# An attention and two-MoE kernel: its first step issued as one hand-ordered piece, with bias rows made on chip

## The chip, the cores and the metric

The kernel runs on one core of a Trainium2 chip. Five engines work in parallel: TensorE (PE in the profile, its weight loads PEld), VectorE (DVE), ScalarE (ACT), GpSimd (POOL) and SyncE (SP), which here issues nearly all transfers. The metric is the device time of one execution in microseconds, lower is better. All data is float32, and the kernel has one launch.

## What is computed

```python
scores = scale * np.matmul(q, k.transpose(0, 1, 3, 2))      # 4 batches, 8 heads, 576 x 576, head dim 64
cum = np.cumsum(np.maximum(s, 0.0), axis=-1)
bias = -(cum[:, :, :, None] - cum[:, :, None, :])
scores = np.where(causal, -1e9, scores + np.minimum(bias, 0.0))
attn = exp(scores - max) / (sum + 1e-9)
x = matmul(attn, v)                                          # then 2304 tokens x 512
h = maximum(maximum(x @ w1, x @ w2), x @ w3) ; x = h @ w_out         # 768 wide
out = ((x @ w_a) * (x @ w_b)) @ w_out2                               # 1536 wide
```

## The kernel before

Attention goes in eight steps: four batches, each in two halves (R = 0: the first 256 query rows, R = 1: the other 320). A step has four pairs of heads; "pair 0" to "pair 3" are those of step 0, "pair 4" to "pair 7" those of step 1, "pair 8" and "pair 9" the first two of step 2. The first three steps are "plain": scores are one matmul of 66 contraction rows, 64 of the head and two that carry the bias. Row 64 of the key operand holds the running sums of `s` (`cum`) and row 65 a constant; the query operand has a constant and `cum`. The host packs the 66-row arrays (`kq0`, `k1`, `q1`) with the constants and a dummy row, and the kernel overwrites the dummy rows.

For one head of step 0 the work is: two score matmuls into a PSUM bank (`f`, line 631), mask and row minimum on VectorE (line 563), exponential with sum on ScalarE (570), two small VectorE operations (574, 575), the division on GpSimd (580), three transposes on TensorE (`ft`, 673), a copy to SBUF (676), and for both heads together eight small matmuls with v (`fpv`, 698). The result is split into a high part on ScalarE (`Xh`, 81) and a low part on VectorE (`Xl`, 92). This is one "unit" of softmax per head, eight units in step 0. Step 1 has per pair one joint tile (`fj`) and four more score tiles.

The first MoE's gates (`g`, 762) follow one step behind: a gate of step 0 is 12 matmuls over the four pairs' `Xh` and `Xl`, so it needs all four. There are 18 weight tiles. Each is loaded as int64 words into `wraw` (512 KB; three buffers) and converted: a Prelu on ScalarE (248), a shift (251) and a combine (252) on VectorE, a copy on GpSimd (`hg`, 88) and a difference on VectorE (`lg`, 92).

The order on each engine is fixed at build time: code is traced in the order of a list of positions (`stream`), under priorities, and a list scheduler with a timeline places each instruction. Every engine then runs its own list in order, and waits where an operand isn't ready. In step 0 pairs 0 and 1 are loaded first, pairs 2 and 3 each behind the bias rows of the pair before (`rows_in`). Dummy matmuls (`spin`, 158) are put between.

Of the kernel before, what the change touches and what calls it, by code (L numbers as in the profile page):

```python
# [8 lines left out]
F32 = mybir.dt.float32  # L9
# [20 lines left out]
def kernel(  # L30
# [48 lines left out]
    def rnd(eng, o, i, scale=1.0):  # L79
        if eng == "A":  # L80
            nc.scalar.activation(o, i, AF.Copy, scale=scale)  # L81
        elif eng == "V":
            if scale == 1.0:
                nc.vector.tensor_copy(o, i)
            else:
                nc.vector.tensor_scalar_mul(o, i, scale)
        else:
            nc.gpsimd.tensor_scalar(o, i, scale, 1.0, op0=ALU.mult, op1=ALU.mult)  # L88

    def sub(eng, o, a, b):  # L90
        e = nc.vector if eng == "V" else nc.gpsimd
        e.tensor_tensor(o, a, b, op=ALU.subtract)
# [42 lines left out]
    SR = s.shape[0]  # L135
# [18 lines left out]
    def spin(n):  # L154

        ps = ps_m.tile([P, 512], F32, tag="m", name="spin")
        for _ in range(n):
            nc.tensor.matmul(ps[:, :P], ident, ident, start=True, stop=True)

    with tc.high_priority(5200):  # L160
        spin(16)

    with tc.high_priority(5000):
        ones = pt_tile([SR, 2, 4 * N1], F32, "ones")[:, 0, : 2 * S]
        cs = pt_tile([SR, 2, 4 * N1], F32, "cs")
        sraw, cum = cs[:, 0, : 2 * S], cs[:, 1, : 2 * S]
        nc.sync.dma_start(sraw, s)
        nc.vector.memset(ones[:, : 2 * S], 1.0)
        nc.vector.memset(ones[:, Q0 : Q0 + 1], 0.0)
        nc.vector.tensor_scalar_max(sraw[:, : 2 * Q0], sraw[:, : 2 * Q0], 0.0)  # L170
# [4 lines left out]
    nc.vector.tensor_scalar_max(sraw[:, 2 * Q0 :], sraw[:, 2 * Q0 :], 0.0)  # L175
    for h in range(2):
        c = slice(2 * Q0 + h * N1, 2 * Q0 + (h + 1) * N1)
        nc.vector.tensor_tensor_scan(
            cum[:, c], ones[:, c], sraw[:, c], cum[:, (h + 1) * Q0 - 1 : (h + 1) * Q0],
            op0=ALU.mult, op1=ALU.add,  # L180
        )

    def store_tails():
        chl = [
            mp.tile([SR, KC * N1], F32R, tag=f"X{c}1", bufs=1, name=f"c{c}")
            for c in "hl"
        ]
        nc.scalar.copy(chl[0][:, : 2 * S], cum)
        nc.gpsimd.tensor_tensor(
            chl[1][:, : 2 * S], cum, f(chl[0][:, : 2 * S]), op=ALU.subtract  # L190
        )
        for (dk, dq, t) in (
            (ck, cq, cum),
            (kt[:, 0], qt[:, 0], f(chl[0])),
            (kt[:, 1], qt[:, 1], f(chl[1])),
        ):
            a, b = parts(t)
            nc.sync.dma_start(dk[:, :, :Q0], a)
            nc.sync.dma_start(dk[:, :, Q0:], b)
            nc.sync.dma_start(dq[:, 0], b[:, 0])  # L200
            nc.sync.dma_start(dq[:, 1, 0:64], b[:, 1, 256:])
            nc.sync.dma_start(dq[:, 1, 64:], b[:, 1, :256])


    KB1 = ap_.tile([P, 2, S], F32R, name="KB1")
    KB2 = ap_.tile([P, 2, S], F32R, name="KB2")
    QA1 = ap_.tile([P, QW], F32R, name="QA1")
    QA2 = ap_.tile([P, QW], F32R, name="QA2")
# [4 lines left out]

    def preset():
        nc.gpsimd.memset(f(QA1[:, N1 : N1 + 64]), 0.0)
# [57 lines left out]
    w1_raw = {}  # L273

    def fetch_w1(key):
        raw = wst.tile([P, WC, 2], I32, tag="wst", name="wraw")
# [9 lines left out]
    def load_w1(key):  # L286
# [8 lines left out]
        with tc.issue_after(done_sm[-1][0]), tc.issue_after(done_sm[-1][1]):  # L295
# [165 lines left out]
    rows_in = []  # L461

    def load_pair(b, p, R):
# [9 lines left out]
        if b == 0 and p >= 2 and R == 0 and plain:  # L473
            t = vo_tile("kqv")[:, : MF * N1]
            kt_, qt_ = t[:, : 4 * Q0], t[:, 4 * Q0 :]
        else:
            kt_ = ap_.tile([P, WK], F32, tag="sk", bufs=2, name="kraw")
            qt_ = kt_ if own and plain else ap_.tile([P, WQV], F32, tag="sq", bufs=2, name="qvraw")
        kn = kt_[:, : 2 * nk]
        if plain and R == 0:  # L480
            qn, vn = kt_[:, 2 * nk : 4 * nk], qt_[:, : nb * P]
            nc.sync.dma_start(kt_[0:66, : 4 * nk], kq0[bp])
# [9 lines left out]
        if plain:  # L492
            if R:
                nc.sync.dma_start(kn[0:66], k1[bp])
                nc.sync.dma_start(qn[0:66], q1[bp])
                nc.sync.dma_start(kn[64:65], ck[bp : bp + 1])
                nc.sync.dma_start(qn[65:66], cq[bp : bp + 1])
            else:
                row = parts(cum)[0][bp : bp + 1] if b == 0 else ck[bp : bp + 1, :, :Q0]
                nc.sync.dma_start(kn[64:65], row)  # L500
                rows_in.append(nc.sync.dma_start(qn[65:66], row).ins)
            nc.sync.dma_start(vn, qv[b, p][:, 2 * nq :])
        else:
            if own:
                nc.sync.dma_start(qt_[:, : 2 * nq], qv[b, p][:, : 2 * nq])
                nc.sync.dma_start(vn, qv[b, p][:, 2 * nq :])
            else:
                nc.sync.dma_start(qt_[:, : 2 * nq + nb * P], qv[b, p])
            for r in (0, 64):
                nc.sync.dma_start(kn[r : r + 64], kT[b, p, :, :, 0:nk])  # L510
# [37 lines left out]
    def softmax(rows, pt, scale):  # L548


        n = len(rows)
        sm = small("sm", 2)
        rs = small("rs", 2)
        for g, parts in enumerate(rows):
            nm = small("nm", 2)
            first = 3.0e38
            for i, (v_, c0) in enumerate(parts):
# [5 lines left out]
                nc.vector.tensor_tensor_reduce(  # L563
# [9 lines left out]
            )  # L573
# [1167 lines left out]
```

## Time and profile before

| | us |
|---|---|
| median of 3 runs | 901.45 (901.07 to 904.96) |
| profiled execution, its own time | 903.33 |
| span of its instructions | 901.5 |
| TensorE busy in the span | 886.2 |
| VectorE busy | 624.9 |

The profiled execution is 1.88 us above the median; 1.83 us of its time lie around the span. TensorE is busy for 98% of the span, but that counts dummy matmuls, and matmuls at the lower of its two clock levels, as full work. The rows below show the first 44 us, where the two differ most from useful work, and the start of step 2 around 105 us.

### The profile page before, as it was taken

To read this page: it belongs to the slowest core of one execution; us is meant where nothing else is said; L and a number is where in the kernel's file an instruction comes from. 1 tells how busy PE (TensorE), PEld (TensorE's weight loads), DVE (VectorE), ACT (ScalarE), POOL (GpSimd) and SP (SyncE) were. 2 spreads that over 40 slices of the span, in tenths; PEclk is the share of its full clock that TensorE was granted. 3 is DMA by queue.
4 is the path that set the end of the run, shared out by engine and by line. 5 is a ranking of instruction groups with operands and counts; after the bars stand their busy time and mean duration, and the time that the engine had idled before them with its cause. 6 is when DMAs were issued, how large, how long until landed. Compare 5 with 4: busy or idle time off the path is not lost.

```text
span 901.5 us, 16886 instructions
## 1 busy us (share of the span) xinstructions
PE 886.2 (98%) x6098; PEld 840.1 (93%) x6098; DVE 624.9 (69%) x1427; ACT 392.8 (44%) x855; POOL 211.1 (23%) x324
## 2 busy tenths in 40 slices
PE   7999999999999999999999999999999999999998
PEld 6677699999999899889999999999999999999998
DVE  4786345677577666647587967767675868987874
ACT  3655455667556556535564322322222223433321
POOL 6552222324233322200001212111111210321211
PEclk8999899999999999999999999999999999999999
DMA  5665253336421873345501014444443245254231
GB/s 186 213 202 191 75 146 101 108 96 189 123 76 55 234 236 128 125 172 201 189 27 71 36 67 152 148 149 146 146 150 120 100 143 165 83 165 153 96 117 47
DMA packets 68267, 120.04 MB, mean 133 GB/s; under 512 B 7016, under 2 KB 50696, under 8 KB 68184
## 3 DMA queue, kind: packets, MB, share of 16 engines
q1 hardware_dynamic: 61272, 111.88, 38.1%
q10 hardware_dynamic: 6912, 7.08, 2.3%
q8 instruction: 48, 0.79, 0.4%
q14 instruction: 35, 0.29, 0.1%
HBM read 87.90 MB, written 31.01 MB: 132 GB/s over the span
## 4 chain that ended last, share of the span: by engine, by line
PE 89%; DMA 5%; DVE 2%; SPq 1%; issue 1%; ACT 1%; POOL 1%; ACTq 0%; DVEq 0%; POOLq 0%
PE X L1107 28%; PE g L762 22%; PE Z L1107 14%; PE Y L1107 7%; PE fpv L698 5%; PE t L714 3%; PE f L631 2%; PE s L587 2%; PE s L588 1%; PE W L1107 1%; PE ft L673 1%; PE tj L727 1%; PE sj L622 1%; PE sj L621 1%; DMA h1S<-st 1%
## 5 line engine op out<-in xcount | busy, mean ns | idle before, releaser
L762 PE MATMUL g<-Xh,lg 128*128 128x256 f32 (+1 forms) x576 | 173.8, 303 | 0.0
L762 PE MATMUL g<-Xh,hg 128*128 128x256 f32 (+1 forms) x576 | 173.2, 305 | 0.5 <-ACT hf L768 0.4
L762 PE MATMUL g<-Xl,hg 128*128 128x256 f32 (+1 forms) x576 | 172.6, 301 | 0.0
L762 PEld LDWEIGHTS g<-Xh,hg 128*128 128x128 f32 x576 | 108.1, 189 | 4.7 <-issue 2.1
L762 PEld LDWEIGHTS g<-Xl,hg 128*128 128x128 f32 x576 | 108.7, 189 | 2.5 <-issue 0.9
L762 PEld LDWEIGHTS g<-Xh,lg 128*128 128x128 f32 x576 | 108.7, 189 | 2.1 <-issue 1.4
L88 POOL TENSOR_SCALAR wh<-wval 128x256 fp32r<-128x256 f32 x77 | 39.8, 527 | 278.8 <-DVE wval L328 229.3
L1107 PE MATMUL X<-xh,wh 128*128 128x384 f32 x288 | 97.3, 338 | 0.1
L1107 PE MATMUL X<-xl,wh 128*128 128x384 f32 x288 | 96.9, 336 | 0.0
L1107 PE MATMUL X<-xh,wl 128*128 128x384 f32 x288 | 96.8, 337 | 0.0
L1107 PE MATMUL X<-woh,slot 128*128 128x256 f32 x408 | 76.6, 281 | 0.5 <-ACT ob L1154 0.5
L580 POOL TENSOR_SCALAR P<-P,rs 128x128 f32<-128x128 f32 (+2 forms) x80 | 49.6, 625 | 99.7 <-DVE rs L575 74.3
L341 DVE TENSOR_TENSOR slot<-hraw,slot 128x768 fp32r<-128x768 f32 x60 | 60.4, 1032 | 13.8 <-POOL slot L88 11.1
L341 DVE TENSOR_TENSOR u<-Z,u 128x384 f32<-128x384 f32 x72 | 39.6, 552 | 37.4 <-ACT u L1154 27.7
L1107 PEld LDWEIGHTS X<-woh,slot 128*128 128x128 f32 x408 | 64.3, 189 | 0.7 <-ACT ob L1154 0.7
L570 ACT ACTIVATE P<-P,nm 128x128 f32<-128x128 f32 (+2 forms) x80 | 46.5, 582 | 33.3 <-DVE nm L563 25.3
L1107 PE MATMUL X<-wol,slot 128*128 128x256 f32 x204 | 56.9, 280 | 0.0
L771 DVE TENSOR_TENSOR hf<-g,hf 128x256 f32<-128x256 f32 (+1 forms) x96 | 43.5, 453 | 17.1 <-PE g L762 12.3
L1107 PEld LDWEIGHTS X<-xh,wh 128*128 128x128 f32 x288 | 54.1, 188 | 0.9 <-ACT s L1148 0.4
L81 ACT ACTIVATE slot<-hraw 128x768 fp32r<-128x768 f32 x39 | 32.5, 846 | 51.4 <-DVE hraw L341 24.4
L1107 PEld LDWEIGHTS X<-xl,wh 128*128 128x128 f32 x288 | 54.1, 188 | 0.0
L1107 PEld LDWEIGHTS X<-xh,wl 128*128 128x128 f32 x288 | 54.0, 188 | 0.0
(199 smaller groups left out, 2234.6 us busy)
## 6 DMA issues: line engine op xcount, KB each, us to landing
hT<-u SPq DMA_DIRECT2D x72, 192.0 KB
hraw<-hT SPq DMA_DIRECT2D x36, 384.0 KB
wraw<-in_moe_w_dram SPq DMA_DIRECT2D x18, 512.0 KB
wraw<-in_moe_w_out_dram SPq DMA_DIRECT2D x18, 512.0 KB
kraw<-in_kT_dram SPq DMA_DIRECT2D x24, 288.0 KB
wraw<-in_moe_w_a_dram SPq DMA_DIRECT2D x12, 512.0 KB
wraw<-in_moe_w_b_dram SPq DMA_DIRECT2D x12, 512.0 KB
st<-h1T SPq DMA_DIRECT2D x24, 192.0 KB
```

The source lines that it names most:

```text
L81: nc.scalar.activation(o, i, AF.Copy, scale=scale)
L88: nc.gpsimd.tensor_scalar(o, i, scale, 1.0, op0=ALU.mult, op1=ALU.mult)
L341: return {"V": nc.vector, "P": nc.gpsimd}[e].tensor_tensor(o, a, b, op=op)
L570: e_ = nc.scalar.activation(pt[:, c0:c1], pt[:, c0:c1], AF.Exp, bias=first, scale=-1.0, accum_out=sm[:, g : g + 1],)
L580: nc.gpsimd.tensor_scalar(pt[:, c0:c1], pt[:, c0:c1], rs[:, g : g + 1], 1.0, op0=ALU.mult, op1=ALU.mult,)
L587: nc.tensor.matmul(ps, QA1[:, qs], KB1[:, h, ksl], start=True, stop=False)
L631: nc.tensor.matmul(o, qn[0:66, h, q0 : q0 + m], kn[0:66, h, k0:k1], start=True, stop=True)
L698: e_ = nc.tensor.matmul(ps[h * D : h * D + D, c0:n], w, x, start=(t == 0), stop=(t == len(mm[h]) - 1),)
L714: nc.tensor.transpose(ps[:, j * P : j * P + P], pt[:, j * P : j * P + P], ident)
L762: nc.tensor.matmul(ps[:, :n], w[:, kk, :], x[:, kk, :], start=(i == 0), stop=(i == len(mm) - 1),)
L771: st["V"] = nc.vector.tensor_tensor(hf, ps[:, :n], hf, op=ALU.max)
L1107: e_ = nc.tensor.matmul(ps[:, :n], w, x, start=(first and i == 0), stop=(i == len(mm) - 1), skip_group_check=not first,)
```

## The change

- **Operands of step 0.** `lead_load` loads all four pairs' 64 head rows at once. Four copies of `s` are loaded to partitions 64 to 127 (two on SP's queue, two on ScalarE's), the running sums are made there, and the bias comes into the operands by multiplication with columns of the identity (keys, on VectorE or GpSimd) and by scaled copies (queries, on ScalarE). The score matmuls contract over 128 rows. The eight one-row transfers from `cum` are gone.
- **Order of step 0.** `lead_in` issues loads, softmax, transposes and products in one written order; `on_pe` chains the TensorE instructions. A unit's sum and division (`sm_b`) come behind the next unit's mask (`sm_a`). Half of the `PF` copies go to VectorE. Weight conversions start behind pair 1's result.
- **Dummy matmuls.** 10 at the start and one later, in place of 48 (96 pieces in the profile, two for each matmul).
- **Weights.** Five tiles are loaded ahead instead of three; two borrow the buffers of later `X` tiles.
- **Later pairs.** Rows 0 to 63 and each of the rows 64 and 65 are loaded by transfers of their own, in a set order (`pair_dma`).
- **Moved.** The stores of the sums for steps 3 and later, and the GpSimd presets of `KB` and `QA`, go into step 1.

```diff
-    SR = s.shape[0]
+    SR = B * NP
...
+    up, rr = slice(64, P), slice(64, 64 + SR)
+    with tc.high_priority(5100):
+        for a, e in enumerate((nc.sync, nc.scalar, nc.sync, nc.scalar)):
+            e.dma_start(sraw[64 + a * SR : 64 + (a + 1) * SR, : 2 * Q0], s[:, : 2 * Q0])
...
         nc.vector.tensor_tensor_scan(
-            cum[:, : 2 * Q0], ones[:, : 2 * Q0], sraw[:, : 2 * Q0], 0.0,
+            cum[up, : 2 * Q0], reset[up], sraw[up, : 2 * Q0], 0.0,
...
-        with tc.issue_after(done_sm[-1][0]), tc.issue_after(done_sm[-1][1]):
+        m = w_behind or done_sm[-1]
+        with tc.issue_after(m[0]), tc.issue_after(m[1]):
             conv_w(raw, hi, lo)
...
             if R:
-                nc.sync.dma_start(kn[0:66], k1[bp])
-                nc.sync.dma_start(qn[0:66], q1[bp])
-                nc.sync.dma_start(kn[64:65], ck[bp : bp + 1])
-                nc.sync.dma_start(qn[65:66], cq[bp : bp + 1])
+                pair_dma(kn[0:64], k1[bp, 0:64])
+                pair_dma(qn[0:64], q1[bp, 0:64])
+                pair_dma(kn[64:65], ck[bp : bp + 1])
+                pair_dma(kn[65:66], k1[bp, 65:66])
+                pair_dma(qn[64:65], q1[bp, 64:65])
+                pair_dma(qn[65:66], cq[bp : bp + 1])
...
+    def lead_in():
...
+            for p in LP:
+                (nc.vector if p < 2 else nc.gpsimd).tensor_scalar(
+                    kk[p][hi_r], cum[hi_r, : 2 * Q0], ident[hi_r, 96 + p : 97 + p], 1.0,
+                    op0=ALU.mult, op1=ALU.mult,
+                )
+                nc.scalar.activation(
+                    qq[p][lo_], cum[lo_, : 2 * Q0], AF.Copy, scale=-float(D) ** 0.5
+                )
...
+            fs(0)
+            fs(1)
+            with tc.issue_after(pend[-1][-1]):
+                scan_tails()
+            store_sums(ck, cq, cum)
+            fs(2)
+            ts(0)
+            fs(3)
+            sm_b(pend.pop(0))
+            ts(1)
+            pv(0)
+            fetch(NP)
+            ts(2)
+            pv(1)
+            fetch(NP + 1)
+            ts(3)
+            wn()
+            pv(2)
+            wn()
+            sp(1)
+            pv(3)
+            wn(NL - 2)
```

TensorE in step 0, before: an excerpt of its list from pair 1's first scores on. `f_N` is a head's score bank, `F_N` its probabilities, `kraw` and `kqv` are operand buffers.

```order
L631 MATMUL f_305<-kraw 128x128
L631 MATMUL f_305<-kraw 128x256
L158 MATMUL spin<-ident 128x128 x4
L631 MATMUL f_397<-kqv 128x128
L631 MATMUL f_397<-kqv 128x256
L631 MATMUL f_326<-kraw 128x128
L631 MATMUL f_326<-kraw 128x256
L158 MATMUL spin<-ident 128x128 x6
L673 MATMUL ft_272<-ident,F_212 128x128 x3
```

TensorE in step 0, after, from the same kind of place (pair 1's second head, then pair 2) to the first transposes.

```order
L1096 MATMUL f_260<-kraw 128x128
L1096 MATMUL f_260<-kraw 128x256
L1096 MATMUL f_284<-kqv 128x128
L1096 MATMUL f_284<-kqv 128x256
L1096 MATMUL f_300<-kqv 128x128
L1096 MATMUL f_300<-kqv 128x256
L710 MATMUL ft_317<-ident,F_217 128x128 x3
L710 MATMUL ft_322<-ident,F_229 128x128 x3
```

The dummy matmuls between are gone, and three pairs' scores stand in a row ahead of the first transposes. In the whole list before, 21 gate matmuls, four `fj` matmuls and three wider score matmuls of step 1 stand ahead of pair 3's last `fpv`; after, none does.

VectorE before, in the middle of step 0 (weight conversion between two heads' masks):

```order
L251 TENSOR_SCALAR wraw<-wraw 128x512
L563 ISA F_327,nm<-f_326,maskJ 128x256
L563 ISA nm 128x1
L92 TENSOR_TENSOR lg_0_159<-wraw,hg_0_158 128x512
L252 SCALAR_TENSOR_TENSOR wraw<-wraw 128x512
L574 TENSOR_SCALAR rs<-sm 128x2
```

VectorE after, from the last unit's sum to the third conversion (`ft_423` is pair 3's second transposed head):

```order
L615 RECIPROCAL rs<-rs 128x2
L92 TENSOR_TENSOR Xl<-fpv,Xh 128x256
L258 TENSOR_SCALAR wraw<-wraw 128x512
L259 SCALAR_TENSOR_TENSOR wraw<-wraw 128x512
L713 COPY PF<-ft_423 128x384
L92 TENSOR_TENSOR Xl<-fpv,Xh 128x256
L258 TENSOR_SCALAR wraw<-wraw 128x512
L92 TENSOR_TENSOR lg_0_141<-wraw,hg_0_140 128x512
L259 SCALAR_TENSOR_TENSOR wraw<-wraw 128x512
```

The conversions moved from among the masks to behind pair 1's result, and the first stands ahead of the copy that pair 3's products wait for.

SP's queue before, around pair 9's operand loads (`kq` is the 66-row operand array, `ck` the stored sums):

```order
L505 DMA qvraw<-in_qv_dram 128x640
L482 DMA kraw<-in_kq_dram 66x1024
L500 DMA kraw<-ck 1x2x256
L501 DMA kraw<-ck 1x2x256
L508 DMA qvraw<-in_qv_dram 128x1280
```

SP's queue after, for pair 9 and ahead of it:

```order
L244 DMA wraw<-in_moe_w_out_dram 128x1024 x2
L557 DMA QA_854<-qt 2x2x320
L553 DMA KB_852<-kt 2x1152
L492 DMA kraw<-in_kq_dram 64x1024
L492 DMA kraw<-ck 1x2x256
L492 DMA kraw<-in_kq_dram 1x512 x2
L492 DMA kraw<-ck 1x2x256
L492 DMA vraw<-in_qv_dram 128x256
```

The sums' rows no longer overwrite what the large load writes; two one-row loads are new, and two weight loads stand ahead.

## Rows read from the trace of the kernel before

**Rows 1.** The page: busy time, share of the span, instructions of each engine.

```profile
PE 886.2 (98%) x6098; PEld 840.1 (93%) x6098; DVE 624.9 (69%) x1427; ACT 392.8 (44%) x855; POOL 211.1 (23%) x324
```

**Rows 2.** Stretches: length, busy per engine (pieces), granted clock, DMA share, GB/s.

```profile
8.26:16.00 7.74, 4.16 (x29) 3.87 (x30) 3.36 (x19) 3.84 (x14) 5.49 (x7) 0.97 0.60 179
...
16.00:22.00 6.00, 6.00 (x25) 5.64 (x26) 2.56 (x8) 0.72 (x2) 1.46 (x3) 0.50 0.83 281
...
16.00:27.00 11.00, 11.00 (x55) 9.28 (x55) 5.36 (x20) 4.15 (x12) 3.45 (x6) 0.71 0.76 241
...
44.20:60.00 15.80, 15.63 (x108) 12.65 (x109) 13.73 (x42) 10.09 (x25) 8.54 (x10) 1.00 0.57 169
```

**Rows 3.** The same for the dummy matmuls of line 158 alone (PE, PEld).

```profile
0.00:44.20 44.20, 15.73 (x96) 15.19 (x96) 0.92 0.63 203
```

**Rows 4.** TensorE and VectorE in order of time: start, length, line, [idle before <-releaser].

```profile
4.41 1.29 DVE L171 TENSOR_TENSOR_SCAN cs<-ones,cs 16x512 f32<-16x512 f32 x1
8.29 0.68 PE L631 MATMUL f<-kraw 66*128 66x128 f32 x4 [0.89 <-DMA kraw<-cs]
...
15.83 1.62 PE L631 MATMUL f<-kqv 66*128 66x128 f32 x4 [3.55 <-DMA kqv<-in_kq_dram]
...
43.32 0.87 PE L698 MATMUL fpv<-PF,kqv 128*64 128x256 f32 x8
```

**Rows 5.** The chain that ended last, first 57 us: start, length, what.

```profile
0.73 2.35 DMA cs<-in_s_dram
...
8.94 4.37 DMA kqv<-in_kq_dram
...
49.30 0.64 PE fj L631 x4
49.94 3.07 PE g L762 x24
...
53.44 0.65 PE f L631 x2
...
55.64 0.86 PE f L631 x2
```

**Rows 6.** Groups by shape, first 45 us: count | busy, mean ns | idle before.

```profile
L248 ACT ACTIVATE wraw<-wraw 128x512 f32<-128x512 f32 x9 | 6.1, 679 | 6.2 <-DMA wraw<-in_moe_w_dram 6.2
L252 DVE SCALAR_TENSOR_TENSOR wraw<-wraw 128x512 int32<-128x512 int32 x8 | 5.7, 710 | 0.0
L580 POOL TENSOR_SCALAR F<-F,rs 128x256 f32<-128x256 f32 x8 | 5.3, 663 | 0.0
L92 DVE TENSOR_TENSOR lg<-wraw,hg 128x512 fp32r<-128x512 f32 x7 | 5.2, 739 | 1.0 <-POOL hg L88 0.8
L251 DVE TENSOR_SCALAR wraw<-wraw 128x512 int32<-128x512 int32 x9 | 4.1, 459 | 2.3 <-DMA wraw<-in_moe_w_dram 2.3
L570 ACT ACTIVATE F<-F,nm 128x256 f32<-128x256 f32 x8 | 4.0, 504 | 0.4 <-DVE nm L563 0.4
L676 ACT COPY PF<-ft 128x384 f32<-128x384 f32 x8 | 3.8, 472 | 4.1 <-PE ft L673 2.1 <-PE fpv L698 2.0
L570 ACT ACTIVATE F<-F,nm 128x128 f32<-128x128 f32 x8 | 3.2, 398 | 3.1 <-DVE nm L563 2.6 <-DVE rs L575 0.5
```

**Rows 7.** TensorE at the start of step 2, columns as in rows 4.

```profile
105.80 0.55 PE L714 MATMUL t<-ident,F 128*128 128x128 f32 x3 [0.67 <-POOL F L580]
107.91 1.62 PE L631 MATMUL f<-kraw 66*128 66x128 f32 x4 [1.56 <-DMA kraw<-ck]
109.46 4.52 PE L698 MATMUL fpv<-PF,qvraw 128*64 128x320 f32 x20
```

**Rows 8.** The chain there, columns as in rows 5.

```profile
101.66 3.08 DMA kraw<-in_kq_dram
...
105.36 2.42 DMA kraw<-ck
```

**Rows 9.** The stretch behind it, columns as in rows 2.

```profile
108.00:114.00 6.00, 6.00 (x25) 2.91 (x25) 1.21 (x8) 1.03 (x5) 1.69 (x5) 0.50 0.34 120
```

More of the change, by code (lines that the diff above doesn't have):

```diff
@@ L157, in spin @@
         for _ in range(n):
[L158 to L170, printed above, removed]
+            last_pe[:] = [
+                nc.tensor.matmul(ps[:, :P], ident, ident, start=True, stop=True).ins
+            ]
@@ L183, in store_tails @@
-    def store_tails():
[L184 to L202, printed above, removed]
@@ L205, with scan_tails @@
[L205 to L208, printed above, removed]
+    def scan_tails():
+        nc.vector.tensor_scalar_max(sraw[rr, 2 * Q0 :], sraw[rr, 2 * Q0 :], 0.0)
+        for h in range(2):
+            c = slice(2 * Q0 + h * N1, 2 * Q0 + (h + 1) * N1)
+            nc.vector.tensor_tensor_scan(
+                cum[rr, c], ones[rr, :N1], sraw[rr, c],
+                cum[rr, (h + 1) * Q0 - 1 : (h + 1) * Q0],
+                op0=ALU.mult, op1=ALU.add,
+            )
@@ L273 @@
     w1_raw = {}
+    w_behind = []
     def fetch_w1(key):
-        raw = wst.tile([P, WC, 2], I32, tag="wst", name="wraw")
+        n = w1_keys.index(key) if key in w1_keys else 0
+        if n in (3, 4):
+            raw = mp.tile([P, KC, N1], I32, tag=f"X{'hl'[n - 3]}1", bufs=1, name="wraw")
+            raw = raw.rearrange("p k c -> p (k c)")[:, : 2 * WC]
+            raw = raw.rearrange("p (c t) -> p c t", t=2)
+        else:
+            raw = wst.tile([P, WC, 2], I32, tag="wst", name="wraw")
         if key[0] == "g":
@@ L459, in is_plain, with lead_load, pair_dma @@
         return 2 * b + R < NPLAIN
-    rows_in = []
+    def lead_load(p):
+        if p < 2:
+            kt_ = ap_.tile([P, 2 * S], F32, tag="sk", bufs=2, name="kraw")
+            qt_ = ap_.tile([P, 2 * N1 + 5 * P], F32, tag="sq", bufs=2, name="qvraw")
+        else:
+            t = vo_tile("kqv")[:, : MF * N1]
+            kt_, qt_ = t[:, : 4 * Q0], t[:, 4 * Q0 :]
+        nc.sync.dma_start(kt_[0:64, : 4 * Q0], kq0[p, 0:64])
+        return kt_[:, : 2 * Q0], kt_[:, 2 * Q0 : 4 * Q0], qt_[:, : 2 * P]
+    NCH, lead_ld = 54, []
+    def pair_dma(dst, src):
+        with tc.issue_after(lead_ld[-1]) if lead_ld and len(lead_ld) < NCH else nullcontext():
+            lead_ld.append(nc.sync.dma_start(dst, src).ins)
     def load_pair(b, p, R):
@@ L472, in load_pair @@
         WK, WQV = 2 * S, 2 * N1 + 5 * P
[L473 to L478, printed above, removed]
+        kt_ = ap_.tile([P, WK], F32, tag="sk", bufs=2, name="kraw")
+        qt_ = kt_ if own and plain else ap_.tile([P, WQV], F32, tag="sq", bufs=2, name="qvraw")
         kn = kt_[:, : 2 * nk]
@@ L633, in f_mm, with f_unit0 @@
         )
-    def f_unit0(kn, qn, h, idle):
-        if idle and h:
-            ps = ps_m.tile([P, 512], F32, tag="m", name="f0")
-        else:
-            ps = ps_s.tile([P, 512], F32, tag="s", name="f0")
+    def f_unit0(kn, qn, h):
+        ps = ps_s.tile([P, 512], F32, tag="s", name="f0")
         pt = ap_.tile([P, S], F32, tag="P", bufs=4, name="F0")
@@ L965 @@
         att = []
-        for p in range(NP):
+        for p in range(NP if stp else 0):
             att += attn_pieces(stp * NP + p, lambda stp=stp: x_tiles(stp))
-        tot = sum(c for c, _ in att)
+        tot = sum(c for c, _ in att) or 1.0
         acc = 0.0
@@ L981, with behind_sm @@
             acc += c
[L983 to L988 removed]
+    def behind_sm(fn):
+        with ExitStack() as es:
+            for e_ in done_sm[-1]:
+                es.enter_context(tc.issue_after(e_))
+            fn()
+    stream.append((1.3, 0, lambda: behind_sm(store_tails)))
+    stream.append((1.6, 0, lambda: behind_sm(preset)))
     def w_next():
@@ L994 @@
     ng = 3 * MF
-    for j in range(ng):
-        w_at = W0[j] if j < 3 else W0[3] + (W1 - W0[3]) * (j - 3) / (ng - 3)
-        stream.append((w_at, 200, w_next))
+    for j in range(NL, ng):
+        stream.append((W0 + (W1 - W0) * (j - NL) / (ng - NL), 200, w_next))
     ns = len(side_keys)
```

187 lines of the change are left out of this document (137 added, 50 removed).

## The prediction

> **What bounds the kernel now.** I read the page first: TensorE is busy for 886.2 of 901.5 us [rows 1], so from step 1 on a change can win only time in which TensorE is idle, runs dummies or runs at its lower clock. The stretches of the first 44 us show where that is. [...] The waits name the cause: pair 1's second head comes at 8 to 16 us behind row transfers, and pair 2 waits 3.55 us for its 66-row load [rows 4], which the chain shows as one transfer of 4.37 us [rows 5]. It was put behind the bias rows of the pair before.
>
> The last product of step 0 ends at 43.32 + 0.87 = 44.19 us [rows 4]. By then TensorE has also done 21 gate matmuls, four `fj`, one 384-wide and two 512-wide score matmuls. From start to start a gate matmul takes 3.07 / 24 = 0.128 us, two `fj` 0.64, the wider ones 0.65 and 0.86 [rows 5]: 2.7 + 1.3 + 0.65 + 1.7 = 6.4 us. If all of step 0 had been done first, steps 1 and later would thus have started at 44.2 - 6.4 = **37.8 us**. From there to the end of step 1 TensorE is nearly full (15.63 of 15.80 us from 44.2 to 60 [rows 2]). The question is what takes the place of 37.8. A second loss stands at the start of step 2: waits of 0.67 and 1.56 us [rows 7], then six us at clock 0.50 [rows 9].
>
> **The new start, step by step.** Launch to sums: a load of `s` takes 2.35 us [rows 5]; the second of SP's copies is issued about 0.4 us behind the first, so the last lands near 3.6 us. The maximum (no longer than a shift over 512 columns, 0.46 [rows 6]) and the scan (1.29 [rows 4]) bring it to 5.3. ScalarE then has four scaled copies of 512 columns; the nearest row is the Prelu over 512, 0.68 [rows 6]. They end near 8.1, the first pair's at 6.0 to 6.4. First scores at about 6.4, against 8.29 now [rows 4].
>
> Eight softmax units: ScalarE needs 0.40 + 0.50 us and one 0.1 to read the sum for each, three `PF` copies of 0.47 [rows 6] and one `Xh`. 8.1 + 8 x 1.0 + 1.8 = 18 us is the lower end for the last exponential. VectorE has about 1.05 us a unit, and in the middle the tails of the sums: 0.5 for the maximum, and two scans of 320 columns, by width 0.8 each from 1.29 for 512 [rows 4]; then its own `PF` copies and `Xl`. Walked through in the written order that puts the last exponential at 19.6 us. I take it, since the scans stand ahead of a reciprocal that GpSimd waits for. Behind it: reciprocal and division 1.5 (GpSimd 0.66 for the wide half [rows 6]), transposes 0.45, the copy 0.47 and, ahead of it on VectorE, a conversion's shift and combine (0.46 + 0.71 [rows 6], half of it under the transposes), products 0.87 [rows 4]. That ends at 24.0 us.
>
> Loads: 4.4 MB stand ahead of pair 4's (four operand sets, v, five weight tiles), 4.8 MB with its k and q. At 241 GB/s (16 to 27 us [rows 2]) from 2.5 us that takes 20 us; with a one-row transfer behind (2.42 [rows 8]) pair 4 is complete near 25. At 300 GB/s it would be 21. So the loads arrive just as the products end. I take **25 us** for the first matmul of step 1, between 23.5 and 28: the upper end has 0.25 us more a unit for waits between the engines, and transposes and products at half clock for part of the way.
>
> What comes back later: up to the first `tj`, TensorE has `fj`, 60 gate matmuls and three score matmuls, 1.3 + 7.7 + 2.4 = 11.4 us. VectorE has in the same stretch four and a half conversions of 0.46 + 0.71 + 0.74 = 1.91 us [rows 6], 8.6 us, and four units' masks and three gate maxima, some 3.8 together: 12.4. These conversions now hide under step 0's waits; afterwards they lie on the path, and I put 1.5 us of gate stalls on it for this stretch and the next, between 0 and 6. VectorE was at 13.73 of 15.80 us after 44.2 [rows 2], so there is room, but not much. The lower clock: it fell after the idle stretch to 16 us and came back after some six us of full work [rows 2]. In the new order the gaps between transposes are up to 2 us, so it may fall near 17 us and be low when step 1 begins; half of up to 6 us, 0 to 3, I take 1.5. The presets moved into step 1 cost GpSimd some 4 us there, between tiles that TensorE needs only some 60 gate matmuls later; nothing, unless GpSimd is late by over 7 us.
>
> Step 0 and 1 together: 37.8 - 25 - 1.5 - 1.5 = 9.8 us won.
>
> **Start of step 2.** Pair 9's buffer comes free when pair 7's last scores are done. Now a 3.08 us load must land before the two rows that overwrite it are sent, 2.42 us for the last [rows 8]. In the new order the rows don't touch what the load writes, so all go out at once: about 2.0 us of issuing and 2.42, 4.4 instead of 6.2. That takes most of the 1.56 us wait [rows 7]. If the clock then stays up, half of the six us [rows 9] is won too. Two bounds, 0 (a weight load lands ahead of it in the queue) and 1.6 + 3.0; I take 2.2. [...]
>
> Removing spins costs or wins nothing beyond this: where TensorE ran them it had nothing else to do. From step 3 on the lists of both kernels are alike.
>
> **Sum.** 9.8 + 2.2 = 12.0 us. The profiled execution of 903.33 would become 891.3; that execution lies 1.88 us above the median of 901.45, which becomes **889.5 us**.
>
> **Rivals.**
> - *Loads hold step 1.* Pair 4's one-row loads stand behind five weight tiles. At the 179 GB/s of 8 to 16 us [rows 2], 4.8 MB take 27 us and step 1 starts near 31; stalls shrink, since conversions run meanwhile. 37.8 - 31 - 1 + 2 = 8: about 894; with a second such wait for pair 5, 898. Against it: that stretch was slow because SP waited to issue.
> - *VectorE becomes the bound of step 1.* Some 13 conversions of 1.91 us are still to be done at 25 us, 25 us of VectorE's time beside masks. If gates stall by 6 to 8 us rather than 1.5, the result is 894 to 896. For it: VectorE is the fullest engine but TensorE there. Against it: with full slots it still has less to do than TensorE.
> - *The clock stays low (slower).* Place: from the lead-in through the first gates. A TensorE that waits for conversions between gates isn't continuously busy, and without dummies nothing fills the holes. [...] The other terms win about 13.5 us, so from 27 us at the lower level on it is a loss; if it lasts until the weights are converted at about 62 us, 18.5 us are lost: 906. For it: both drops of now follow stretches with idle time [rows 2, 7, 9]. Against it: both ended after some six us of steady work. [...]
> - *The lead-in doesn't shorten as meant.* If each unit waits for the one before (mask, exponential, sum, division, about 2.5 us in a row), eight need 20 us and step 1 starts near 32 to 35: with stalls 898 to 900.
>
> **How the numbers follow.** The forecast, 12 us won with terms between 7 and 18 (883 to 895): 0.66. Loads 0.12, VectorE 0.12, clock 0.05, no shorter lead-in 0.05. The lowest corner, start at 23.5, no stalls and 4.6 at step 2, is 901.45 - 18.9 = 882.6; it needs every term at its end, so the range begins at 883. It ends at 899, with the loads and most of the last rival inside and the low clock outside. About 0.5%, 4.5 us, is what a measurement of this kernel can tell from no change. Faster by more (under 896.9): nearly all of the forecast, most of VectorE, half of the loads, 0.80. Within: 0.14. Slower by more: 0.06.
>
> **What would show it.** Right: first scores at 6 to 7 us, the last exponential of step 0 at 18 to 21, `fj` at 24 to 28, TensorE over 9 tenths full from there, and at the start of step 2 no wait on `ck` rows over 0.5 us. Wrong: `fj` waiting for a row transfer or for q of pair 4 past 30 us; holes ahead of `g` released by `wraw` or `lg` on VectorE adding to over 5 us between 25 and 65; a clock of 0.50 beyond 32 us.

## The result, and the profile after

The changed kernel takes **886.51 us** (median of 4 runs, 886.17 to 886.75) against 901.52 of the kernel before in the same session. The ratio is 0.9825, with a 95% interval from 0.9801 to 0.9849: 15 us faster. The profiled execution has a span of 884.6 us, 16.9 less than before. That is more than the medians differ, because the profiled execution of the kernel before lies 1.88 us above its median. Executions of that kernel differ in their mean granted clock: in later sessions they took 897.7 to 899.1 us at 0.998, 902.8 and 904.2 at 0.991, one took 962.5 at 0.847, and the profiled one has 0.992. What follows on the clock holds for the profiled executions.

The page of the changed kernel, busy time and share of each engine [rows 1], then the granted clock in 40 slices:

```profile
PE 870.1 (98%) x6024; PEld 828.3 (94%) x6024; DVE 631.4 (71%) x1437; ACT 393.4 (44%) x859; POOL 209.7 (24%) x327
...
PEclk9999999999999999999999999999999999999999
```

TensorE is busy for 16.1 us less and idle for 0.8 us less (14.5 against 15.3). So the gain is not idle time; it is busy time that did nothing useful. The groups of TensorE by line (line, operation, count | busy, mean ns | idle before) say which, first those of the kernel before, then of the changed one:

```profile
L631 PE MATMUL f<-kraw 66*128 66x128 f32 (+1 forms) x48 | 11.9, 374 | 2.4 <-DMA kraw<-ck 1.6 <-DMA kraw<-cs 0.9
L631 PE MATMUL f<-kqv 66*128 66x128 f32 (+1 forms) x16 | 3.9, 386 | 3.5 <-DMA kqv<-in_kq_dram 3.5
```

```profile
L710 PE MATMUL ft<-ident,F 128*128 128x128 f32 x48 | 9.5, 285 | 2.7 <-POOL F L619 1.8 <-DVE rs L614 0.4 <-DVE PF L713 0.2
L671 PE MATMUL f<-kraw 66*128 66x128 f32 (+1 forms) x32 | 6.4, 333 | 0.0
L159 PE MATMUL spin<-ident 128*128 128x128 f32 x22 | 4.4, 376 | 2.0 <-POOL ident masks.py:199 2.0
L1096 PE MATMUL f<-kqv 128*128 128x128 f32 (+1 forms) x16 | 2.9, 327 | 0.0
L1096 PE MATMUL f<-kraw 128*128 128x128 f32 (+1 forms) x16 | 2.9, 334 | 0.3 <-ACT kraw L1072 0.3
```

Dummies fell from 15.7 us [rows 3] to 4.4. The 64 score pieces of steps 0 and 2 take 6.4 + 2.9 + 2.9 = 12.2 us, and the same groups of the kernel before take 11.9 + 3.9 = 15.8 us. The transposes take 9.5 instead of 10.4, and the products over `qvraw` 26.0 instead of 29.9, while the gates take 522.4 instead of 519.6. Groups overlap in time, so they can't be added up; the mean granted clock of the span can: 0.998 instead of 0.992 means 1.8 us of work lost to the lower level instead of 7.2. With the dummies that is 11.3 + 5.4 = 16.7, against 16.1 (each clock is rounded to a thousandth, some 0.4 us either way). So the gain is dummies gone, and work no longer done at half clock. Contracting over 128 rows instead of 66 costs nothing that shows: 327 to 334 ns a piece in both forms.

TensorE of the changed kernel in step 0, in order of time [rows 4]:

```profile
6.29 2.89 PE L1096 MATMUL f<-kraw 128*128 128x128 f32 x16 [0.34 <-ACT kraw L1072]
...
13.84 0.89 PE L710 MATMUL ft<-ident,F 128*128 128x128 f32 x3 [0.66 <-POOL F L619]
15.59 0.89 PE L710 MATMUL ft<-ident,F 128*128 128x128 f32 x3 [0.86 <-POOL F L619]
...
22.32 0.87 PE L737 MATMUL fpv<-PF,kqv 128*64 128x256 f32 x8
23.01 1.15 PE L671 MATMUL fj<-kraw,qvraw 66*64 66x288 f32 x8
```

Step 1 begins at 23.01 us with no wait. The stretches (length, then busy time of each engine, granted clock, DMA share, GB/s), as [rows 2]:

```profile
8.26:16.00 7.74, 5.67 (x32) 3.98 (x30) 7.18 (x35) 5.82 (x26) 4.07 (x8) 1.00 1.05 388
16.00:24.00 8.00, 7.18 (x56) 4.24 (x56) 6.68 (x23) 5.50 (x17) 3.93 (x9) 1.00 0.65 175
24.00:32.90 8.90, 7.64 (x50) 6.05 (x49) 8.90 (x22) 3.13 (x7) 3.76 (x4) 1.00 0.66 220
32.90:44.20 11.30, 11.21 (x78) 8.73 (x77) 10.15 (x32) 7.43 (x18) 6.62 (x9) 1.00 0.49 148
44.20:60.00 15.80, 15.28 (x108) 11.31 (x107) 14.57 (x39) 10.12 (x24) 6.68 (x8) 1.00 0.71 223
60.00:80.00 20.00, 19.73 (x135) 15.39 (x136) 15.91 (x49) 11.66 (x28) 12.94 (x18) 1.00 0.65 200
80.00:101.50 21.50, 21.48 (x143) 16.24 (x142) 10.36 (x56) 13.89 (x46) 7.45 (x15) 1.00 0.40 118
101.50:116.00 14.50, 14.50 (x104) 14.10 (x104) 7.58 (x23) 6.92 (x19) 3.20 (x7) 1.00 0.87 237
```

In these stretches the clock is never below 1.00, where it was 0.50 before from 16 to 22 us [rows 2] and from 108 to 114 us [rows 9]. VectorE is full from 24 to 32.9 us, and there TensorE misses 1.26 us.

### The profile page after: what moved, and what is told of

The parts are those of the page before. It is cut to its first block, busy times and chain, and to the rows that moved or that the text cites. A ratio compares the mean times of both kernels' runs of the same rounds, so it can differ in the third digit from the quotient of the medians.

```text
span 884.6 us, 16783 instructions
## 1 busy us (share of the span) xinstructions
PE 870.1 (98%) x6024; PEld 828.3 (94%) x6024; DVE 631.4 (71%) x1437; ACT 393.4 (44%) x859; POOL 209.7 (24%) x327
## 4 chain that ended last, share of the span: by engine, by line
PE 92%; DVE 4%; DMA 2%; ACT 1%; issue 1%; POOL 1%; SPq 0%; ACTq 0%; DVEq 0%; POOLq 0%
PE X L1252 29%; PE g L803 24%; PE Z L1252 15%; PE Y L1252 8%; PE fpv L737 5%; PE t L755 3%; PE s L627 2%; PE s L628 2%; PE f L671 1%; PE W L1252 1%; PE ft L710 1%; PE tj L768 1%; DVE lg L92 1%; PE sj L662 1%; PE sj L661 1%
## 5 line engine op out<-in xcount | busy, mean ns | idle before, releaser
L803 PE MATMUL g<-Xh,hg 128*128 128x320 f32 (+1 forms) x576 | 175.7, 308 | 0.7 <-POOL hg L88 0.5
L598 DVE CUSTOM_DVE_ANT_0 P<-s,maskJ 128x128 f32<-128x128 f32 (+2 forms) x80 | 40.6, 514 | 19.8 <-PE s L628 12.7
```

Source lines behind the costliest of these rows:

```text
L598: t_ = nc.vector.tensor_tensor_reduce(pt[:, c0 : c0 + w], v_, m_, -scale, first, op0=ALU.add, op1=ALU.min, accum_out=nm[:, i : i + 1],)
L803: nc.tensor.matmul(ps[:, :n], w[:, kk, :], x[:, kk, :], start=(i == 0), stop=(i == len(mm) - 1),)
```

## The experiments

Times below are medians, with the ratio to the kernel before measured in the same session. Most differences among the changed versions are a few us, so the traces carry much of the argument; each trace shows one execution.

### Which part of step 0 wins?

Three versions each leave out something. The first is the kernel before, with all four pairs loaded at once and the weights behind them:

```
-        fetch(1)
-        for i in range(2, NP):
-            with tc.issue_after(rows_in[i - 1]):
-                fetch_w1(w1_keys[i - 2])
-                fetch(i)
-        fetch_w1(w1_keys[2])
+        for i in range(1, NP):
+            fetch(i)
+        for i in range(3):
+            fetch_w1(w1_keys[i])
```

> The kernel before, with one part of the change: the loads of pairs 2 and 3 no longer wait for the bias rows of the pair before; the weight loads come behind all four pairs. Bias rows still go by transfer, and dummies, order rules and later loads are those of before. Theory: the load order is the larger part of the lead-in; pair 2's scores no longer wait for its 66-row load until 15.8 us, and the time is 892 to 896. Rival (the written order and the sums made in place carry the gain): 899 to 902.

902.12 us, ratio 1.0007 (0.9990 to 1.0025): nothing. The 3.55 us wait of pair 2 [rows 4] became others; TensorE in order of time (the profiled execution, 906.47 us, is the slowest of ten):

```profile
17.47 0.89 PE L631 MATMUL f<-kqv 66*128 66x128 f32 x4 [1.69 <-DMA kqv<-cs]
...
28.33 1.16 PE L158 MATMUL spin<-ident 128*128 128x128 f32 x8 [1.52 <-DVE nm L563]
```

Pair 2's first scores come 3.3 us earlier (12.52 us), and yet `fj` begins at 33.84 us instead of 32.90. Behind the load of 4.37 us stood the row transfers, and behind those VectorE, which in this trace waits 4.33 us for a weight tile, with a conversion that stands ahead of the next mask (it is busy for 4.93 of 8.90 us from 24 to 32.9 us).

The second is the changed kernel, order and all, with the bias rows sent by eight one-row transfers as before. Its loads have 66 rows, and its scores contract over 66:

```
-                (nc.vector if p < 2 else nc.gpsimd).tensor_scalar(
-                    kk[p][hi_r], cum[hi_r, : 2 * Q0], ident[hi_r, 96 + p : 97 + p], 1.0,
...
-                nc.scalar.activation(
-                    qq[p][lo_], cum[lo_, : 2 * Q0], AF.Copy, scale=-float(D) ** 0.5
-                )
...
+                nc.sync.dma_start(two(kk[p])[64:65], row0[p : p + 1])
+                nc.sync.dma_start(two(qq[p])[65:66], row0[p : p + 1])
```

> The changed kernel with one part undone: for step 0 the 66-row operands are loaded and the bias rows come by eight one-row transfers from the sums, the twelve operations that make them on VectorE, GpSimd and ScalarE are left out; order, loads at once and later pairs stay. Theory: first scores at 8.0 to 8.5 us instead of 6.3 and pair 3's rows near 12.5, so step 1 starts 1.5 to 3 us later: 888 to 889.5. Rival (the softmax chain hides it, and ScalarE and VectorE are freed of 4 to 5 us of work): 885.5 to 887.

894.54 us, ratio 0.9928 (0.9903 to 0.9953): half of the gain is gone, far more than expected. TensorE's first scores, and the two stretches behind them (TensorE alone):

```profile
9.97 5.39 PE L1086 MATMUL f<-kraw 66*128 66x128 f32 x16 [3.31 <-DMA kraw<-eKB]
```

```profile
8.26:16.00 7.74, 6.03 (x19) 0.62 0.54 168
16.00:24.00 8.00, 7.40 (x26) 0.50 0.65 247
```

The first scores come 3.7 us later, and run at the lower clock: 16 pieces take 5.39 us, not 2.89. To tell the two apart, the same version got 19 dummies instead of 10, to cover the wait:

> The version with the bias rows by eight one-row transfers (894.5 us; its operations that make the rows on the operands' partitions are left out), with 19 dummy matmuls instead of 10, so that TensorE is busy until close to its first scores at 9.97 us. Theory: of the 8 us that this version lost, half is the later start and half the lower clock behind the idle stretch from 6 to 10 us; with the stretch filled the first 16 score pieces take about 3 us instead of 5.4, the clock stays at 1.00 to 24 us, and the time is 890 to 891.5. Rival: the clock isn't what costs, or it falls later anyway in the waits for single rows: 893.5 to 895.

891.54 us (0.9886, 0.9866 to 0.9906). The pieces take 2.86 us again, which gives back 3 us. The expectation of 890 to 891.5 was right in kind, but not that the clock would hold: it fell later, in the same kind of holes as in the changed kernel (0.65 and 0.61 us behind the division).

```profile
10.44 2.86 PE L1086 MATMUL f<-kraw 66*128 66x128 f32 x16 [1.13 <-DMA kraw<-eKB]
...
17.85 1.14 PE L710 MATMUL ft<-ident,F 128*128 128x128 f32 x3 [0.65 <-POOL F L619]
19.60 1.14 PE L710 MATMUL ft<-ident,F 128*128 128x128 f32 x3 [0.61 <-POOL F L619]
```

So of the 8 us that transfers cost here (9.3 by the ratios), the dummies give back 3 (3.8): the clock at the first scores. The other 5 (5.5) are the later start with what follows from it, the later fall of the clock (0.63 from 16 to 24 us) among it. Loads of 66 rows instead of 64, and loads of v and weights that go out some 6 us later, are in these 5 too; no run separates them.

The third has loads at once and sums in place, and step 0 in the order of the kernel before:

```
-        for p in range(NP if stp else 0):
+        for p in range(NP):
...
-        with tc.issue_after(lead_pe[-1]) if i == NP else nullcontext():
+        with nullcontext():
...
-            fs(0)
-            fs(1)
...
-            wn(NL - 2)
```

Attention pieces, dummies and weight conversions are back at their old positions of the list (those lines are not printed here).

> The changed kernel's loads and sums in place, with step 0 in the order of the kernel before: its attention pieces, dummies, weight conversions and their positions come from the old list and the list scheduler, nothing is chained on TensorE, and all copies of the transposed probabilities are ScalarE's. Loads at once alone gave 902.1 us, loads and written order without sums in place 894.5. Theory: each of the two (sums in place, written order) carries part of the gain; conversions and gates between the masks hold back step 0 here, but they aren't lost: 889 to 893, with the last products of step 0 past 30 us and gates ahead of them. Rival one: sums in place bring it all, the written order nothing: 886 to 888. Rival two: the sums in place bring little without the order: 896 to 900.

896.67 us, ratio 0.9962 (0.9949 to 0.9974). This is rival two: sums in place bring little without the order. TensorE has its first scores at 6.44 us here too, but in two stretches it has few pieces and a low clock:

```profile
24.00:32.90 8.90, 7.24 (x29) 0.73 0.81 253
32.90:44.20 11.30, 10.73 (x47) 0.76 0.33 108
```

The last product of step 0 ends after 44 us. The chain that ended last shows what it goes through from 16 to 30 us: VectorE, with conversions between the masks.

```profile
16.45 0.67 DVE wraw L258
17.12 0.06 DVE F L598
...
19.22 0.75 DVE wraw L258 x2
...
21.13 0.59 DVE lg L92
21.72 1.21 DVE wraw L259 x2
```

By ratios on 901.5 us: loads at once +0.6 us, and with sums in place -3.4, and with the written order instead -6.5, with both -15.8. But the last three versions also have the new loads of later pairs, which the first hasn't, so part of their gain lies at step 2. The last wide score tile of step 1 tells the two apart. TensorE in the kernel before, with loads at once, with sums in place in the old order, with the written order and transfers, and in the changed kernel:

```profile
100.81 0.81 PE L631 MATMUL f<-kraw,qvraw 66*128 66x384 f32 x2
...
100.43 0.81 PE L631 MATMUL f<-kraw,qvraw 66*128 66x384 f32 x2
...
99.87 0.81 PE L671 MATMUL f<-kraw,qvraw 66*128 66x384 f32 x2
...
97.31 0.81 PE L671 MATMUL f<-kraw,qvraw 66*128 66x384 f32 x2
...
88.00 0.81 PE L671 MATMUL f<-kraw,qvraw 66*128 66x384 f32 x2
```

Up to there the two parts win 0.9 and 3.5 us alone, and 12.8 together. The kernel before and the changed one have 234 gate matmuls ahead of that tile, the other two 228 and 230, so alone the parts win a little less still. The rest comes behind it: from 101.5 to 116 us TensorE is full at clock 1.00 in both versions (14.50 of 14.50 us), where the kernel before has 12.27 us at 0.76. So step 0 is short only when both are there. The traces name the two things that hold it, row transfers in one version and conversions between the masks in the other. No run separates what the conversions' new place, the `PF` copies on VectorE, or the moved stores and presets win.

### Is it the chain on TensorE?

```
-        with tc.issue_after(lead_pe[-1]) if lead_pe else nullcontext():
-            out_ = fn()
+        out_ = fn()
```

> The changed kernel without the chain that fixes TensorE's order in step 0; everything else is as it is, and the list scheduler may put the score matmuls, transposes, products and gates in its own order. Theory: the chain is worth little, because the order in which step 0 is written already gives the scheduler nearly the same list (scores first, then transposes); only two gate matmuls get ahead of the last products and would wait for the third pair's split: 886 to 888 us, fj within 1 us of 23.0. Rival: the fixed order carries a good part of the gain, since a gate matmul ahead of the products holds the whole engine: 890 to 894, with a wait over 2 us ahead of a gate before 30 us.

887.98 us (0.9840, 0.9815 to 0.9865): at the upper end of the theory, though `fj` comes at 24.81 us in the profiled execution (889.85, the slowest of four), not within 1 us of 23.0. The order in which the code is written does nearly all of the work; fixing it on TensorE adds some 1.5 us by the medians, which lies inside the interval.

### The dummies

```
-            spin(10)
...
-            sp(1)
```

> The changed kernel without its eleven dummy matmuls. Theory: with scores and transposes close together real work alone keeps the clock up; 886 to 887, granted clock 1.00 from 6 to 25 us. Rival (the clock needs the dummies): a granted clock of 0.50 in several us between 6 and 25 and later steps shifted by 1 to 4 us, 887.5 to 890.5.

887.83 us (0.9858, 0.9833 to 0.9883), 1.3 us above the changed kernel by the medians, though nothing waits for dummies. That is less than the intervals can tell, but the trace sides with the rival:

```profile
6.31 5.10 PE L1095 MATMUL f<-kraw 128*128 128x128 f32 x16 [6.31 <-ACT kraw L1071]
...
24.99 1.17 PE L671 MATMUL fj<-kraw,qvraw 66*64 66x288 f32 x8
```

TensorE, idle for 6.31 us before, runs its first 16 pieces in 5.10 us instead of 2.89, step 1 begins 2 us later, and the clock is 0.79 from 16 to 24 us.

### The rows of later pairs

Later pairs load 66 rows again and overwrite two:

```
-                pair_dma(kn[0:64], k1[bp, 0:64])
+                pair_dma(kn[0:66], k1[bp])
...
-                pair_dma(kn[65:66], k1[bp, 65:66])
```

> The changed kernel, but pairs 4 and later load 66 rows at once and then overwrite two of them, as the kernel before does (four or five transfers a pair instead of six or seven). Theory: the gain at the start of step 2 comes from these loads. Then pair 9's scores wait about 1 to 2 us for a ck row again, the granted clock falls to 0.50 for some six us behind that, and the median is 890 to 892 (886.5 + 4 to 5). Rival: the start of step 2 improved because the order ahead of it is another one; then no wait over 0.5 us there, clock 1.00, and 886 to 887.5.

888.04 us (0.9857, 0.9831 to 0.9882). TensorE at the start of step 2 and its stretches there:

```profile
94.29 1.55 PE L667 MATMUL f<-kraw 66*128 66x128 f32 x8 [0.95 <-DMA kraw<-ck]
103.61 0.89 PE L667 MATMUL f<-kraw 66*128 66x128 f32 x4 [1.09 <-DMA kraw<-ck]
```

```profile
80.00:101.50 21.50, 20.55 (x137) 1.00 0.24 76
101.50:116.00 14.50, 13.41 (x94) 1.00 0.87 234
```

There are two waits again, both for a `ck` row, 2.04 us together against 2.23 before [rows 7], but the clock stays at 1.00 where it fell to 0.50 for six us [rows 9]. So the row split itself is worth 1.5 us by the medians (2.9 by the ratios, which this many runs don't tell apart), and 2.0 us of idle time in the trace; the other 3 us, half of six us at the lower clock, came back without it. Why two such waits were followed by the lower clock before and not here is open: they are further apart here (9.3 us against 2.1), and the longer one is 1.09 us instead of 1.56. It need not be the waits alone: the version with loads at once waits 1.71 and 1.58 us for `ck` rows there and has 1.00 from 101.5 to 116 us, and the kernel before has executions at a mean clock of 0.998.

### What still holds the changed kernel

ScalarE waits 1.92 us for a mask in the middle of step 0, behind the rest of the running sums on VectorE. This version moves these behind later masks, and their maximum to GpSimd:

```
             fs(1)
+            fs(2)
             with tc.issue_after(pend[-1][-1]):
                 scan_tails()
...
-        nc.vector.tensor_scalar_max(sraw[rr, 2 * Q0 :], sraw[rr, 2 * Q0 :], 0.0)
+        nc.gpsimd.tensor_scalar_max(sraw[rr, 2 * Q0 :], sraw[rr, 2 * Q0 :], 0.0)
```

> The changed kernel with the rest of the running sums (a maximum of 16 x 640 and two scans, 2.3 us on VectorE) moved from behind pair 1's masks to behind the first mask of pair 2's second head and later, and the maximum put on GpSimd. Theory: in the changed kernel these hold back a mask for which ScalarE waits 1.92 us in the middle of its exponentials; with it gone the last exponential ends 1 to 1.5 us earlier, fj begins at 21.8 to 22.3, and the time is 885 to 886. Rival: the sums are then stored later, pair 4's one-row loads from them come after the products, and fj waits for them: 886.5 to 888.

889.06 us (0.9860, 0.9837 to 0.9883): 2.5 us above the changed kernel by the medians, and by neither theory. GpSimd, then VectorE:

```profile
9.47 1.80 POOL L185 TENSOR_SCALAR eKB<-eKB 16x640 f32<-16x640 f32 x1 [1.94 <-DMA eKB<-in_s_dram]
11.36 2.44 POOL L619 TENSOR_SCALAR F<-F,rs 128x128 f32<-128x128 f32 x6
```

```profile
12.83 0.29 DVE L598 CUSTOM_DVE_ANT_0 F<-f,maskJ 128x128 f32<-128x128 f32 x1 [1.33 <-PE ft L710]
```

The maximum, 0.52 us on VectorE, takes 1.80 on GpSimd, just ahead of the divisions. These come late, so the transposes do, and VectorE's next mask waits 1.33 us for one of the four buffers that the transposes free. The hole was moved, not closed. The version makes two edits at once, so what the later place alone would do isn't shown.

The next two versions change how many weight tiles are loaded and converted ahead of step 1, to three and then to two:

```
-    NL, W0, W1 = 5, 1.0, 1.5
+    NL, W0, W1 = 3, 1.0, 1.5
```

> The changed kernel with three weight tiles loaded ahead instead of five; the other two are asked for only when the conversions reach them. Theory: the loads ahead of pair 4 are not what sets the start of step 1 (fj had no wait on a transfer), so fj stays at 23 us, and the fourth and fifth tile come later, behind the loads of pair 4 and 5: gates wait for them, 2 to 5 us in all, 888 to 891 us. Rival: the five tiles crowd out pair 4's loads and are needed late anyway: 885.5 to 887.

**883.07 us** (882.14 to 884.11), ratio 0.9792 (0.9769 to 0.9814): below both kernels, and by neither theory. Against the changed kernel it is 3.4 us by the medians and 3.0 by the ratios, whose intervals overlap a little. All five loads are still issued by 12 us; what moves is VectorE. The mask of step 1's joint tile has two parts. With five tiles the second part comes at 29.24 us, behind conversions; with three at 27.74, though `fj` itself begins 0.8 us later there:

```profile
27.59 1.73 DVE L259 SCALAR_TENSOR_TENSOR wraw<-wraw 128x512 int32<-128x512 int32 x2
29.24 0.50 DVE L598 CUSTOM_DVE_ANT_0 FJ<-fj,maskJ,nm 128x288 f32<-128x288 f32 x1
```

(changed kernel) and, with three tiles ahead,

```profile
27.74 0.51 DVE L598 CUSTOM_DVE_ANT_0 FJ<-fj,maskJ,nm 128x288 f32<-128x288 f32 x1
```

TensorE is then idle for 1.3 us from 24 to 100 us instead of 2.2. The larger part lies elsewhere: the wait for `QA` (below), which ends at 291.5 us here and at 293.8 in the changed kernel, is 1.0 us instead of 2.2, and the clock stays up behind it.

> The changed kernel with two weight tiles loaded and converted ahead of step 1's first softmax instead of five. Theory: what three instead of five won lies on VectorE: the conversions that stand ahead of step 1's first mask hold back its softmax, and gates have enough converted tiles to go on with. Two leave one conversion less ahead of that mask (some 1.9 us), but from the third tile on gates would wait for conversions: about as with three, 882.5 to 884.5. Rival: it was the order of loads, or the stall at 291 us, that changed by chance, and the number ahead has no steady effect: back at 886 to 888.

885.37 us (0.9821, 0.9797 to 0.9846): between. Two are too few for TensorE, which is idle 2.1 us from 24 to 100 us. With differences of 1 to 3 us the runs don't settle the best number.

The wait for `QA` is one that the changed kernel lengthened; the waits of TensorE (line, releaser: total, times, longest) have, before and after:

```profile
PE s L588 <- DMA QA<-kt: 1.2, 1, 1.2
...
PE s L628 <- DMA QA<-kt: 2.2, 1, 2.2
```

On SP's list that load stands behind a staging load (`st`) in both kernels. The next version exchanges the two, with three weights ahead:

```
-        at = (5.95, 7.12)[k // KM] + ...
+        at = (6.02, 7.12)[k // KM] + ...
```

> The version with three weight tiles converted ahead of step 1 (883.1 us), and the second of the staging loads of h1T placed a little later in the list (6.02 instead of 5.95), so that on SP's queue it stands behind the load of sums into QA that it now stands ahead of. Theory: the wait of TensorE for QA near 291 us (1.0 us here, 2.2 us in the changed kernel) is the time that this load spends behind a staging load that waits for a buffer; with the two exchanged the wait goes and the time is 881.5 to 882.5. Rival: the load is late for another reason, or a later load takes its place with the same wait: 883 to 884.

886.86 us (0.9830, 0.9806 to 0.9854): the rival, only worse. The wait for `QA` is gone; 20 us later TensorE waits longer. A staging load goes out at 303.06 us, VectorE stands from 302.9 to 309.3 us ahead of the sums over what it brings (the profile puts the end of that down to a load behind it on the queue), and the mask is queued behind those (VectorE, then TensorE):

```profile
309.31 1.74 DVE L356 TENSOR_TENSOR st<-st 128x384 f32<-128x384 f32 x3 [6.42 <-DMA kraw<-in_kT_dram]
310.97 0.45 DVE L598 CUSTOM_DVE_ANT_0 PJ<-sj,maskJ 128x288 f32<-128x288 f32 x1
```

```profile
311.48 0.69 PE L627 MATMUL s<-KB,QA 128*128 128x384 f32 x1 [3.14 <-DVE nm L598]
```

The clock is 0.66 from 310 to 320 us behind that. The time goes with such clocks: the one execution with a mean clock of 0.998 took 885.14 us, the three at 0.994 and 0.995 took 886.8 to 887.2. The last version adds to this one dummy in each of the two holes of step 0:

```
+                if p == 1:
+                    sp(1)
                 on_pe(tr)
```

> The version with the staging load later, and one dummy matmul put into each of the two holes of TensorE near 13 and 15 us, ahead of pair 1's transposes, where it waits 0.66 and 0.86 us for the division. Theory: these holes are what lets the granted clock fall to 0.79 between 16 and 24 us in some executions; filled, it stays at 1.00 and fj begins 0.5 to 0.8 us earlier: 0.3 to 0.8 us faster than without, 881 to 882. Rival: the dummies push the transposes back by as much, or the clock falls all the same: no faster, 881.8 to 883.

887.45 us (0.9843, 0.9816 to 0.9870): no faster than without. In the profiled execution the clock is 1.00 from 16 to 24 us where it was 0.79, and step 1 begins 0.3 us earlier, at 23.49 instead of 23.83. The dummies don't push the transposes back: these come 0.4 us later (14.32 instead of 13.94 us), but so do the scores ahead of the dummies, whose first 16 pieces took 3.34 us instead of 2.96. That execution is the fastest of four (885.24 us, mean clock 1.000); the others have 0.994 and 0.995, as low as without the dummies, and took 886.8 to 888.2. So one trace with the clock up doesn't show that the dummies keep it up.

## Why the prediction was right, point by point

The forecast of 889.5 us was 3 us too slow, and its mechanism is what the trace shows: the lead-in is shorter by about what was summed, and the wait and the lower clock at step 2 are gone. Its terms are compared here with the profiled executions (16.9 us); by the medians 15.0 us were won.

- **Effective start before, 37.8 us.** This is an estimate, and no run contradicts it: by it, 37.8 - 23.0 = 14.8 us of the 16.9 are won there. One reading under it was off and changes no term: pair 1's second head didn't wait for row transfers. It stands on TensorE's list behind pair 2's first head, and so behind that pair's 66-row load; it ran at 17.24 us.
- **New start, 25 us: 2 us too late.** First scores 6.29 (said 6.4), end of ScalarE's copies 7.80 (8.1), last exponential 18.99 (19.6), products 23.19 (24.0). Each is a little early, and the tails of the sums do hold the exponentials, as walked through. What was too slow besides is the last step, the loads: 241 GB/s was taken from 16 to 27 us, where SP waited to issue too (1.8 us for a buffer), and they ran at 388 from 8.26 to 16 us. Pair 4 was there, and `fj` waited for nothing.
- **Gate stalls, 1.5 us.** TensorE is idle for 2.1 us from 24 to 80 us, released by VectorE and GpSimd as expected. Three tiles ahead show that some of it could be had.
- **Low clock behind the lead-in, 1.5 us.** It didn't fall in the profiled execution, but it was 0.79 from 16 to 24 us in the version with overwritten rows, whose step 0 is the same up to 16 us, and in three others; `fj` came at 23.84 there. The term is 0 or 0.8 us, and which of the two differs from trace to trace.
- **Step 2, 2.2 us: too small.** The waits (2.23 us) and the six us at half clock (3.0) both went, 5.2 in all in the profiled executions, beyond the upper end of 4.6. The clock was taken as a bonus that depends on the waits; with rows overwritten it came back beside waits of 2.04 us.
- **"From step 3 on the lists are alike": true of the lists, not of the waits.** The same two transfers on SP met with other timing, and 1.0 us was given back at 294 us, with a clock of 0.83 from 290 to 300 us, which is 1.7 us more.
- **Sum.** 14.8 - 2.1 + 5.2 - 1.0 - 1.7 = 15.2 us of the 16.9 between the spans; the other 1.7 us isn't traced to a place. That the forecast's 12.0 came within 3 us of the medians' 15.0 is in part luck: start, clock and step 2 were too pessimistic by 2, 1.5 and 3 us, the stalls too optimistic by 0.6, and 2.7 us that came back near 294 us weren't in the sum.
- **The signs.** First scores, last exponential and the `ck` rows of step 2 came as said. `fj` came earlier than 24 to 28, and TensorE was not over 9 tenths full at once: 7.64 of 8.90 us from 24 to 32.9, full only behind that. Of the signs of being wrong one came by the letter only, a lower clock beyond 32 us: it is the short one near 295 us, far from the lead-in that was meant.
- **Rivals.** *Loads hold step 1*: no, for the reason above. *VectorE bounds step 1*: the place is right (8.90 of 8.90 us busy from 24 to 32.9), the size is 1.26 us there. *Low clock*: not in this kernel's lead-in, but it is real, and the version with bias transfers had it, 0.62, 0.50 and 0.82 from 8.26 to 32.9 us. That each us at the lower level costs half a us, as the 27 us and the 906 count it, was the author's estimate from a clock of 0.50; no changed version stays there that long (0.988 is the lowest mean clock of an execution), and in the version with bias transfers 16 score pieces took 5.39 us instead of 2.89. *Lead-in doesn't shorten*: not here. The version with the old order comes near its time, but by conversions between the masks, not by units that wait for each other.
- **Removing spins costs nothing beyond this**: not refuted for those removed (two put back into the holes won nothing that shows), but the ten kept at the start do something: without them the first pieces take 2.2 us longer.

## What to carry to other kernels

When an engine is 98% busy, look at what the busy time holds: here dummies and work at half clock were the whole gain, and idle time hardly moved. Removing one of two waits that end together won nothing or little here: loads at once left the time as it was (902.12 us), and on top of them sums in place and the written order gave 0.9 and 3.5 us alone up to the end of step 1, and 12.8 together. When versions share another part of the change, compare them at a point in the trace ahead of it, and not by their whole times. One trace says what the clock did in one execution: look at the mean clock of the others before a fall or its absence is put down to an edit. Before an operation is moved to an idle engine or a transfer behind another, look what stands next in that engine's list: both such moves here cost more than they took away (2.5 and 3.8 us by the medians).

## What the hardware showed that was not expected

- The same holes of 0.66 and 0.86 us between transposes were followed by a clock of 0.79 (16 to 24 us) in four of the five traces that have them (overwritten rows, three and two weights ahead, staging load later) and of 1.00 in one, the changed kernel's. Up to 16 us the traces of overwritten rows and of the changed kernel differ on TensorE by little but the length of the first dummies (4.24 and 3.94 us for the same 20 pieces).
- One kernel, the one before, ran at mean granted clocks from 0.991 to 0.998 in all executions but the one at 0.847; it took 897.7 to 899.1 us at 0.998 and otherwise up to 904.6.
- The clock's row doesn't show the slow pieces at the start of the run without dummies: it reads 1.00 from 8.26 to 16 us and ahead of that, where pieces take 5.10 us for 16 instead of 2.89 (6.31 to 11.41 us).
- A maximum over 16 x 640 elements took 1.80 us on GpSimd (the version with the sums later) and 0.52 on VectorE (the changed kernel).
- Eight one-row transfers took 0.50 to 0.65 us each to issue in the version with bias transfers; the one-row loads of pairs 4 and 5 in the changed kernel took 0.22 to 0.44. The eight kept SP from 5.2 to 10.5 us, and the v and weight loads behind them went out some 6 us later than in the changed kernel (first weight at 12.55 instead of 6.67 us).
